# Loading 104 of 128 rows of keys and queries from the fifth unit of attention on

## The chip, the core and the metric

The kernel runs on one core of one Trainium2 chip, in one launch. The metric is the device time in microseconds (us). The core has a matrix engine (TensorE; PE in the profile, PEld for its weight loads), a vector engine (VectorE, DVE), a scalar engine (ScalarE, ACT), a general engine (GpSimd, POOL) and a queue processor that here only issues transfers (SyncE, SP). All transfers between the chip's memory and the core's own memory of 128 rows run on 16 DMA engines.

## The reference, cut to what matters

Three stages follow one another: a gated linear attention over 4 x 8 heads, 768 steps and 40 numbers a head; a routed layer of 8 experts with a capacity of 384 tokens each; and a dense layer with 2048 hidden units. The change touches the loads of the first.

```python
for t in range(S):
    kt, vt, qt = (k[:, :, t], v[:, :, t], q[:, :, t])
    ...
    C = f_stab[:, :, None, None] * C + i_stab[:, :, None, None] * np.einsum('bhd,bhe->bhde', vt, kt)
    n = f_stab[:, :, None] * n + i_stab[:, :, None] * kt
    h_tilde = np.einsum('bhde,bhe->bhd', C, qt)
    nq = np.einsum('bhd,bhd->bh', n, qt)[:, :, None]
    denom = np.maximum(np.abs(nq), 1.0)
    ...
    y[:, :, t] = o * h_tilde / denom
```

The attention's output, 3072 rows of 320, is routed to one of eight experts a row (`relu(x @ w1) @ w2`), and then goes through `elu(x @ w_in) @ w_out`.

## The kernel before

Attention is cut into 24 units: 12 chunks of 64 steps, times two pairs of batches. A unit holds 16 heads, 8 in the upper 64 rows and 8 in the lower 64 rows of every tile, since a head needs only 40 numbers. Its keys and queries are one tile `qk` of 128 rows x 2 x 8 x 64 numbers (512 KB): rows 0 to 39 carry one batch's 40 dimensions, rows 64 to 103 the other's. The host fills rows 40 to 63 and 104 to 127 with zeros (`_layout`, L1464 and L1465). The product of a unit's keys and queries (`scores`, L284) and of its scaled queries and the state (`recall`, L366) run over all 64 rows of a half, so what stands in those rows has to be zero.

There are four `qk` buffers (`QKb`, L149), used in turn. `load_qk` (L254) issues one transfer on the queue of SP. Units 0 to 3 are loaded at the start, unit 4 after the first scores, unit 5 in step 0. In step u the order of a unit is: 16 products of weights and values alternate on PE with 16 of the scores of unit u+2 (L352, L284); the decay factors of u+2 (L309, L299, L302); the transpose of the output of u-1 (L422); recall and the new state (L366, L378); on POOL the scaled queries of u+1 (`factors`, L316), which is the last reader of that unit's `qk` tile; then the load of unit u+5 into the same buffer, the gates on DVE and POOL (L398 to L406), the logits (L432), two writes of the output to memory (`rows_out`, L416) and the load of values and keys by token of unit u+4 (`load_vk`, L260, 484 KB).

So on SP's queue the transfers stand in a fixed order: two writes `xd`, one `vk`, now and then a piece of the dense layer's first weight (`cx`, L842, which is converted beside attention), one `qk`. A load that has to wait holds back all that stand behind it. The product of scores of unit u+5 comes in step u+3, over two steps after its load was issued. Units' loads number 24; the first four go to fresh buffers.

After attention come the routing rounds and, interleaved with them by a planner that works with fixed costs, the experts and the dense layer (L1081 and L1219 to L1223, the larger part of the time). They read nothing of `qk`.

Of the kernel before, what the change touches and what calls it, by code (L numbers as in the profile page):

```python
# [117 lines left out]
class Attention:  # L118
# [134 lines left out]

    def load_qk(self, u):  # L254
        self.QK[u] = self.QKb[u % 4]
        self.nc.sync.dma_start(self.QK[u], self.qk[u])

    def load_vk(self, u):
        self.VK[u] = self.two.tile([128, 968], F32, name="vk", bufs=6)
# [1237 lines left out]
```

## Time and profile before

| what | us |
|---|---|
| median of 3 runs | 794.91 |
| lowest and highest of them | 784.56, 798.31 |
| the profiled execution's own time | 790.17 |
| its span | 788.4 |

The profile is of one execution, with a mean granted clock of 0.944 for TensorE. It gives each engine's busy time, the share of the DMA engines that is busy, which engine waited for which, and the chain of work that ended last. Attention takes the first 160 us or so of the span, the routing alone some 30 us, the rest of the span is experts and dense layer.

### The profile page before, as it was taken

The numbers are of one execution on the slowest core, as the hardware profiler recorded it, in microseconds if no ns is written. First come the engines' busy times: TensorE is split into PE (matmuls) and PEld (weight loads), VectorE is DVE, ScalarE is ACT, GpSimd is POOL, SyncE is SP. The second block draws the span as 40 slices with busy tenths as digits, with TensorE's granted clock in tenths as the row PEclk, the third lists the DMA queues.
The fourth block names the chain that finished last, engine by engine and source line by source line (L and its number), as shares of the span: only waits on it lengthen the run. The fifth ranks groups of instructions, "written<-read, shape, count | busy, mean of one in ns | idle before, by whom it ended". The sixth has DMA issues, their size and how long they took to land.

```text
span 788.4 us, 18307 instructions
## 1 busy us (share of the span) xinstructions
PE 727.4 (92%) x7379; PEld 668.6 (85%) x7379; DVE 541.2 (69%) x1599; ACT 384.1 (49%) x822; POOL 222.8 (28%) x273
## 2 busy tenths in 40 slices
PE   7889789934999789999999999999999999999995
PEld 4767677823999688999999899999999999999994
DVE  8457657577889966795787579769857843852441
ACT  5545444424456643572565267336625743742452
POOL 4668757625213520121040012112012221001001
PEclk9879978966999889999999999999999999999998
DMA  7767777335212410230050023023002421000000
GB/s 272 240 207 253 248 234 215 94 98 174 92 29 64 154 59 1 74 105 26 1 177 2 25 81 98 26 81 97 1 26 82 135 72 58 35 1 26 1 1 26
DMA packets 24070, 72.80 MB, mean 92 GB/s; under 512 B 3568, under 2 KB 7664, under 8 KB 23984
## 3 DMA queue, kind: packets, MB, share of 16 engines
q1 hardware_dynamic: 15488, 39.80, 16.0%
q0 software_dynamic: 8448, 31.73, 12.3%
q8 instruction: 58, 0.95, 0.5%
q14 instruction: 28, 0.23, 0.1%
q10 hardware_dynamic: 48, 0.10, 0.0%
HBM read 62.96 MB, written 8.65 MB: 91 GB/s over the span
## 4 chain that ended last, share of the span: by engine, by line
PE 59%; issue 19%; POOL 8%; DVE 7%; DMA 3%; ACT 2%; SPq 1%; POOLq 0%; ACTq 0%; DVEq 0%
PE ph L1081 26%; PE acc L1223 5%; PE acc L1219 5%; PE acc L1220 5%; PE acc L1188 3%; PE acc L1190 2%; PE acc L1189 2%; POOL qt L316 2%; PE pr L713 2%; POOL kt L325 2%; POOL C L327 2%; PE acc L1175 1%; DMA qk<-in_qk_dram 1%; PE acc L1177 1%; PE pX L432 1%
## 5 line engine op out<-in xcount | busy, mean ns | idle before, releaser
L1219 PE MATMUL acc<-woh,gh 128*128 128x320 f32 x384 | 121.2, 315 | 1.5 <-ACT woh L958 1.5
L1223 PE MATMUL acc<-woh,gl 128*128 128x320 f32 x384 | 119.8, 312 | 0.7 <-DVE gl L965 0.6
L1220 PE MATMUL acc<-wol,gh 128*128 128x320 f32 x384 | 119.2, 311 | 0.5 <-POOL wol L951 0.5
L1130 ACT ACTIVATE e<-ph 128x384 f32<-128x384 f32 x128 | 62.3, 487 | 89.6 <-PE ph L1081 82.0
L1134 DVE SCALAR_TENSOR_TENSOR e<-e,ph 128x384 f32<-128x384 f32 x128 | 70.2, 550 | 49.7 <-ACT e L1131 49.4
L1081 PE MATMUL ph<-yh,wih 128*128 128x384 f32 x256 | 89.7, 351 | 0.3
L1098 ACT ACTIVATE gh<-ph 128x384 fp32r<-128x384 f32 x64 | 31.4, 490 | 116.6 <-PE ph L1081 100.0
L1081 PE MATMUL ph<-yh,wil 128*128 128x384 f32 x256 | 85.9, 335 | 0.0
L1229 POOL DMA_INDIRECT out_dram<-ot,idx x24 | 23.9, 996 | 202.5 <-ACT ot L958 199.7
L965 DVE TENSOR_TENSOR gl<-e,gh 128x384 fp32r<-128x384 f32 x128 | 73.4, 581 | 1.4
L1219 PEld LDWEIGHTS acc<-woh,gh 128*128 128x128 f32 x384 | 72.8, 190 | 1.8 <-ACT woh L958 1.8
L1223 PEld LDWEIGHTS acc<-woh,gl 128*128 128x128 f32 x384 | 72.6, 189 | 1.9 <-DVE gl L965 1.5
L1105 DVE SCALAR_TENSOR_TENSOR gl<-ph,gh 128x384 fp32r<-128x384 f32 x64 | 35.4, 555 | 56.1 <-ACT gh L1098 56.1
L1220 PEld LDWEIGHTS acc<-wol,gh 128*128 128x128 f32 x384 | 72.6, 189 | 0.8 <-POOL wol L951 0.8
L1131 ACT ACTIVATE e<-e 128x384 f32<-128x384 f32 x128 | 67.3, 526 | 4.1
L1081 PE MATMUL ph<-yl,wih 128*128 128x384 f32 x256 | 66.1, 339 | 0.0
L969 POOL DMA_INDIRECT stg<-in_w1a_dram,wi x16 | 16.3, 1018 | 145.9 <-DVE wi L751 128.2
L958 ACT ACTIVATE gh<-e 128x384 fp32r<-128x384 f32 x95 | 48.4, 515 | 11.2 <-DVE e L1134 11.0
L1081 PEld LDWEIGHTS ph<-yh,wih 128*128 128x128 f32 x256 | 48.3, 189 | 3.7 <-ACT yh L1193 3.6
L1081 PEld LDWEIGHTS ph<-yh,wil 128*128 128x128 f32 x256 | 48.2, 188 | 0.0
L1081 PE MATMUL ph<-xh,w1h 128*128 128x384 f32 x128 | 45.5, 355 | 0.7 <-ACT xh L958 0.6
L1081 PEld LDWEIGHTS ph<-yl,wih 128*128 128x128 f32 x256 | 45.8, 189 | 0.0
(260 smaller groups left out, 1929.7 us busy)
## 6 DMA issues: line engine op xcount, KB each, us to landing
qk<-in_qk_dram SPq DMA_DIRECT2D x24, 512.0 KB, 5.8
vk<-in_vk_dram SPq DMA_DIRECT2D x24, 484.0 KB, 4.5
wx<-in_wout_dram SPq DMA_DIRECT2D x16, 320.0 KB, 2.9
xd<-x SPq DMA_DIRECT2D x48, 96.0 KB, 2.3
cx<-in_win_dram SPq DMA_DIRECT2D x8, 512.0 KB, 5.7
cx<-in_win_dram SPq DMA_DIRECT2D x4, 256.0 KB, 6.4
xg<-xd,idx POOLq DMA_INDIRECT x24, 3.1
out_dram<-ot,idx POOLq DMA_INDIRECT x24, 2.5
```

The source lines that it names most:

```text
L958: self.nc.scalar.activation(out, x, AF.Copy)
L965: self.nc.vector.tensor_tensor(out, x, y, op=ALU.subtract)
L1081: PE.matmul(p, w, x, start=k == 0, stop=k == 7)
L1098: nc.scalar.activation(h, p, AF.Relu)
L1105: nc.vector.scalar_tensor_tensor(l, p, 0.0, h, op0=ALU.max, op1=ALU.subtract)
L1130: nc.scalar.activation(e, p, AF.Relu, scale=-1.0)
L1131: nc.scalar.activation(e, e, AF.Exp, scale=-1.0)
L1134: nc.vector.scalar_tensor_tensor(e, e, -1.0, p, op0=ALU.add, op1=ALU.max)
L1219: PE.matmul(p, h[:, c], self.woh[:, f], start=f == 0, stop=False)
L1220: PE.matmul(p, h[:, c], self.wol[:, f], start=False, stop=False)
L1223: PE.matmul(p, l[:, c], self.woh[:, f], start=False, stop=f == 15)
L1229: s = nc.gpsimd.indirect_dma_start(out=self.out, out_offset=bass.IndirectOffsetOnAxis(ap=idx[:, t:t + 1], axis=0), in_=o, in_offset=None)
```

## The change

From unit 4 on, a load takes rows 0 to 103 of the source and writes rows 0 to 103 of the buffer. Rows 104 to 127 of each of the four buffers keep what the first load wrote there, which is zeros. 20 of the 24 loads become 104 rows of 4096 bytes (416 KB) in place of 128 rows (512 KB). Nothing else changes: every engine has the same instructions in the same order as before, and the transfers wait for the same engines; only the size of these 20 differs.

```diff
     def load_qk(self, u):
         self.QK[u] = self.QKb[u % 4]
-        self.nc.sync.dma_start(self.QK[u], self.qk[u])
+        n = 128 if u < 4 else 104
+        self.nc.sync.dma_start(self.QK[u][:n], self.qk[u, :n])
```

## Rows read from the trace of the kernel before

**Rows 1.** The page: span, busy time of each engine with its share and instructions.

```profile
span 788.4 us, 18307 instructions
...
PE 727.4 (92%) x7379; PEld 668.6 (85%) x7379; DVE 541.2 (69%) x1599; ACT 384.1 (49%) x822; POOL 222.8 (28%) x273
```

**Rows 2.** The page: busy tenths in 40 slices, DMA engines and bytes moved likewise.

```profile
PE   7889789934999789999999999999999999999995
...
DMA  7767777335212410230050023023002421000000
```

**Rows 3.** Busy time by stretch: engines, granted clock, DMA share, GB/s; attention and four pieces.

```profile
core 0: us, PE busy (x) PEld busy (x) DVE busy (x) ACT busy (x) POOL busy (x), PEclk, DMA share, GB/s
15.00:141.00 126.00, 109.46 (x2909) 88.83 (x2908) 79.74 (x183) 61.52 (x141) 86.46 (x85) 0.84 0.71 224
48.00:59.00 11.00, 11.00 (x229) 8.96 (x229) 6.25 (x14) 5.41 (x12) 6.41 (x7) 0.53 0.73 235
59.00:89.00 30.00, 26.28 (x824) 21.40 (x818) 20.77 (x51) 15.35 (x39) 25.78 (x25) 1.00 0.79 257
107.00:117.00 10.00, 9.85 (x205) 8.14 (x208) 4.89 (x10) 4.06 (x11) 5.38 (x6) 0.51 0.84 249
130.00:141.00 11.00, 10.12 (x178) 8.15 (x178) 7.43 (x14) 4.53 (x10) 7.20 (x8) 0.53 0.56 179
```

**Rows 4.** The tile qk: who reads and writes it, when, and who waited for it.

```profile
L256 SPq DMA_DIRECT2D qk<-in_qk_dram x24: 327/390/2152, 1.2 to 132.3; - x24
L316 POOL TENSOR_TENSOR qt<-qk,db x22: 1286/1482/1814, 19.8 to 153.8; 128x512 f32<-128x512 f32 x22
...
who waited for it (us, times):
  PEld pS L284: 0.4, 1
...
DMA to landing us min/median/max: 4.0/5.8/9.2
```

**Rows 5.** SP's queue and PE in time: load of unit 12, its first product.

```profile
63.87 2.15 SPq L256 DMA_DIRECT2D qk<-in_qk_dram  x1
...
75.50 0.28 PE L284 MATMUL pS<-qk 64*64 64x64 f32 x2
```

**Rows 6.** DMA queues (packets, MB, share of 16 engines' span) and issues (KB each).

```profile
q1 hardware_dynamic: 15488, 39.80, 16.0%
...
q8 instruction: 58, 0.95, 0.5%
...
qk<-in_qk_dram SPq DMA_DIRECT2D x24, 512.0 KB, 5.8
vk<-in_vk_dram SPq DMA_DIRECT2D x24, 484.0 KB, 4.5
...
xd<-x SPq DMA_DIRECT2D x48, 96.0 KB, 2.3
cx<-in_win_dram SPq DMA_DIRECT2D x8, 512.0 KB, 5.7
cx<-in_win_dram SPq DMA_DIRECT2D x4, 256.0 KB, 6.4
```

**Rows 7.** The chain that ended last, 15 to 160 us: two of its longest pieces.

```profile
80.01 4.76 DMA qk<-in_qk_dram
105.22 5.17 DMA qk<-in_qk_dram
```

**Rows 8.** POOL in order of time, behind those two pieces of the chain.

```profile
83.28 1.74 POOL L316 TENSOR_TENSOR qt<-qk,db 128x512 f32<-128x512 f32 x1
84.99 1.26 POOL L914 TENSOR_TENSOR wil<-cF,wih 128x512 fp32r<-128x512 f32 x1
...
110.04 0.72 POOL L406 TENSOR_TENSOR x<-x,rd 128x320 f32<-128x320 f32 x1 [2.18 <-DVE x L405]
110.72 1.48 POOL L316 TENSOR_TENSOR qt<-qk,db 128x512 f32<-128x512 f32 x1
```

**Rows 9.** PE's waits, 15 to 160 us: us in total, times, longest.

```profile
PE pS L284 <- issue: 3.7, 3, 2.0
PE pO L352 <- issue: 2.6, 2, 2.5
PE pO L366 <- issue: 2.2, 1, 2.2
...
PE pF L309 <- issue: 1.4, 1, 1.4
```

**Rows 10.** PE in order of time: three of those waits, in brackets.

```profile
47.27 0.27 PE L284 MATMUL pS<-qk 64*64 64x64 f32 x2 [2.04 <-issue]
...
105.05 0.27 PE L352 MATMUL pO<-vk,P 64*64 64x64 f32 x2 [2.46 <-issue]
...
130.88 0.48 PE L284 MATMUL pS<-qk 64*64 64x64 f32 x4 [1.22 <-issue]
```

**Rows 11.** SP's own waits over the whole span.

```profile
SPq L416 <- ACT x L413: 83.5, 23, 6.9
```

## The prediction

> **What bounds the kernel now.** I read the page first. PE is busy for 92% of the span [rows 1], and from slice 19 on for nine tenths of every slice, while the DMA engines fall from seven tenths in the first slices to almost nothing [rows 2]. The experts and the dense layer behind attention are therefore PE's, and no load of keys and queries is left there. The change can act only on the first 155 us or so, and through the time at which attention ends.
>
> Next I read that stage by stretches [rows 3]. From 15 to 141 us no engine is full: PE is busy for 109.5 of 126 us, POOL for 86.5, VectorE for 79.7, and the DMA engines have a share of 0.71 at 224 GB/s. The pace comes from the 22 scaled-query instructions on POOL, the first at 19.8 and the last at 153.8 us [rows 4]: 134.0 / 21 = 6.4 us a unit. [...]
>
> Then I asked the tile itself who waits for its loads. In the whole run one instruction did, for 0.4 us, and it is a product of scores (L284) [rows 4]; the first loads of the program, which the change leaves alone, are those that nothing hides. Loads land 4.0 to 9.2 us after issue, 5.8 in the middle [rows 4]. Against that stands a lead of two steps: the load of unit 12 was held up longest on SP, was issued at 63.87, and its first product ran at 75.50 us [rows 5]. Even the slowest landing of all, 9.2 us, would have been there at 73.1.
>
> One view speaks against this. The chain of waits lists two qk loads, 4.76 and 5.17 us long, as pieces of the chain that ended last [rows 7]. What follows in the first case is POOL's L914, which reads no qk; POOL had been at work until then without a pause, as it had before L316 in the second [rows 8]. No engine stood still for these landings. The chain's steps are inferred from semaphores, and these two lead past an engine that was busy. I count them as no wait; were they real, the shorter load would give at most 24 of 128 rows of 9.9 us, 1.9 us.
>
> **The change, part by part.** It removes 20 x 24 rows of 4096 bytes, 1.97 MB. SP's queue carried 39.80 MB in 16.0% of 16 engines' span [rows 6], 0.16 x 16 x 788.4 = 2018 us of engine time, so 19.7 KB per us and engine. A load of 512 KB costs 26.6 us of engine time, 1.66 us on each of 16 engines; one of 416 KB costs 21.6, 1.35 us on each of 16. That is 20 x 0.31 = 6.2 us in all if the engines were the bound. They are not: at 0.71 they stand idle for more than a quarter of the stage. Its cover is the lead of two steps; were that gone, 0.31 us a unit is what it would be worth.
>
> By the rows an even spread, 1.35 us an engine, is the nearest guess, as every load shown has rows in multiples of 16. [...]
>
> SP issues the same number of transfers in the same order. Its issue of a qk load takes 390 ns in the middle [rows 4], and SP stands for 83.5 us of the run in front of the output's writes, waiting for ACT [rows 11]; even twice the 390 ns would disappear there. The engines' instructions and operands have the same shapes, so nothing is added to PE or POOL.
>
> What remains is contention. PE waits 9.9 us in this stage for nothing that the profile shows (3.7 + 2.6 + 2.2 + 1.4) [rows 9], in a few pieces of 1 to 2.5 us in the midst of products whose inputs are there; three stand in [rows 10], at 47, 105 and 131 us. Each of these three comes just before or at the start of a stretch at half clock. Those stretches hold 229 + 205 + 178 = 612 matmuls in 32 us, which take 22.3 us at 27.5 per us: 9.7 us lost. The DMA engines also carry 58 instruction packets, 0.95 MB, 0.5% of 16 engines' span [rows 6], so 16 KB and 1.1 us each, and these share the engines with the loads. [...]
>
> The price of less contention is bounded by 0 and by 9.9 + 9.7 = 19.6 us. The stage moves 24 x 512 + 24 x 484 + 48 x 96 + 8 x 512 + 4 x 256 = 33,632 KB [rows 6], and 20 x 96 = 1920 KB go, 5.7%. I take that share of the bound, 1.1 us, since only so much of the traffic leaves. Below nothing is not excluded either: where these waits fall differs from run to run, and the three runs of one program lie 13.75 us apart.
>
> **The sum.** 790.2 us of the profiled execution, less 1.1, is 789.1. That execution is 4.7 us under the median of the runs shown; from the median it is 793.8. I predict the middle of both, **792 us**.
>
> **Rivals.** [...]
>
> *The DMA engines are the bound after all.* Then the even spread gives 6.2 us, 784. Against it: the single wait of 0.4 us, and the lead. It lies within the forecast's range.
>
> *The 104 rows go to few engines, and the load becomes the bound.* All else takes 0.71 x 6.4 - 1.66 = 2.9 us of each engine a unit. With k engines the load adds 21.6 / k, and the unit grows once 2.9 + 21.6 / k passes 6.4, below k = 6.2. At 13 engines it is 4.6 and at 8 it is 5.6, both hidden; at 4 it is 8.3, and 1.9 us more for each of 20 units end at 828 us; one engine would give some 1,150. For it: no transfer with such a count of rows is shown. Against it: 104 can be cut evenly in 13 or 8 parts, and nothing in the rows confines a transfer to four.
>
> *The waits fall worse.* The same contention with other timing adds two or three waits of 2 us with their slow stretches, 6 to 14 us: 796 to 804, which is also the upper half of what the runs show.
>
> **How the numbers follow.** Forecast 0.80, with a range of its own of 781 to 802, which is the spread of the runs around it with the bounds of the small terms. PE's waits gone (under 781) 0.09, few engines 0.05, worse waits beyond 802 0.06. 2% of the median, 15.9 us, is about what a measurement of this kernel can tell from no change; it puts the limits at 779 and 811. Of the first rival 0.07 lies under 779; of the last 0.01 lies over 811, with the 0.05 of few engines. So faster 0.07, same 0.87, slower 0.06. The range 778 to 804 leaves out the far ends of each.
>
> **What would show it.** The qk load's time to landing should stay between 4 and 9 us, with 5 or so in the middle, and nobody should wait for it beyond the start. The DMA share from 15 to 141 us should fall by a few hundredths, not the unit's 6.4 us. [...] Only a stage that gets shorter while no wait of PE's has changed would break the reasoning as a whole.

## The result and the profile after

The change makes the kernel a little slower: 797.93 us in the median of 20 runs (792.7 to 803.8) against 795.01 us of before (20 runs, 784.56 to 800.89), ratio 1.0063 with a 95% interval of 1.0038 to 1.0087. The ratio leaves out seven runs of before that took over 1.5% longer than its fastest, and none of the change; over all 20 and 20 the medians stand at 1.0037, the means at 1.0037 with an interval of 1.001 to 1.0066. I had forecast a little faster.

The profiled execution took 799.42 us, its span is 797.7 us, 9.3 us longer than before. The medians differ by 2.9 us only, so the two profiles show more than the change costs. PE's busy time is that of [rows 1], 727.8 against 727.4 us.

The tile qk and its users (as [rows 4]): count, shortest, middle and longest in ns, first and last start in us.

```profile
L257 SPq DMA_DIRECT2D qk<-in_qk_dram x24: 318/366/1409, 1.2 to 140.4; - x24
L317 POOL TENSOR_TENSOR qt<-qk,db x22: 1281/1484/1753, 19.4 to 162.0; 128x512 f32<-128x512 f32 x22
...
who waited for it (us, times):
busy tenths in 40 slices 9999999900000000000000000000000000000000
```

The last scaled-query instruction starts at 162.0 in place of 153.8 us: 8.2 of the 9.3 us were lost inside attention. Nobody waited for a qk load; before, one instruction did, for 0.4 us [rows 4]. The lead of two steps held, so the loss did not come by a late load.

PE's waits from 15 us to the end of attention (as [rows 9]): us in total, times, longest.

```profile
PE pC L379 <- issue: 6.8, 3, 2.9
PE pS L285 <- issue: 6.0, 3, 3.1
PE pO L367 <- issue: 5.0, 3, 2.2
PE pD L310 <- issue: 3.2, 1, 3.2
...
PE pO L353 <- issue: 1.0, 2, 0.8
```

The waits for nothing that the profile shows went from 9.9 us (10.3 with two of 0.2 us that [rows 9] does not show) to 22.0 us. In these two executions that is the whole loss, and more. Three of them in order of time, with the wait in brackets:

```profile
49.46 0.37 PE L285 MATMUL pS<-qk 64*64 64x64 f32 x2 [3.14 <-issue]
...
77.43 0.53 PE L310 MATMUL pD<-fp,sel 96*128 96x64 bf16 x7 [3.19 <-issue]
...
120.38 0.43 PE L379 MATMUL pC<-vk,kt 64*40 64x64 f32 x2 [2.88 <-issue]
```

They are not only more but longer: 3.1 and 3.2 us where the longest in [rows 9] was 2.5.

The DMA queues (as [rows 6]) and the stretch 15 to 141 us (as [rows 3]; the last three numbers are granted clock, DMA share and GB/s):

```profile
q1 hardware_dynamic: 14948, 37.83, 16.5%
```

```profile
15.00:141.00 126.00, 99.73 (x2696) 81.18 (x2695) 74.62 (x173) 56.97 (x132) 81.79 (x80) 0.85 0.72 201
```

This is the surprise. SP's queue moved 1.97 MB less and kept the engines busy for longer: 0.165 x 16 x 797.7 = 2106 us of engine time against 2018, 55.7 us per MB against 50.7. In the same 126 us the DMA share is 0.72 (before 0.71) at 201 GB/s (before 224), and PE got 2696 matmuls done in place of 2909, at a granted clock of 0.85 against 0.84. So it is not the clock.

The packets' own records in the trace say which ones became slow. All 4096-byte packets of SP's queue (qk and cx) and the 3872-byte ones (vk), from 16 us to the end of attention:

```
                 4096 bytes: mean ns, share over 200 ns     3872 bytes: mean ns
before           179, 0.11                                  209
change           221, 0.46                                  211
```

The 3872-byte packets, of loads that were not cut, stay as they were. The 4096-byte ones are those of qk and cx together. Counted off in the order of the issues, which is an estimate where two transfers overlap, qk's took 173 ns before and 232 after, cx's 189 and 203, and cx's smaller packets of 1024 bytes 74 and 96. So the cut loads became slower most, and cx a little with them.

The queue has 540 packets fewer (14948 against 15488), the 480 rows and three more for each of the 20 loads. These three are packets of 4 bytes: 2016 of them before, 16 for each of the queue's 126 transfers, and 1956 after, so 13 for a load of 104 rows. I take them for one on each engine that carries rows of the load, 13 engines in place of 16; that is an estimate from these counts, since no record names its engine. The trace also has 40 completions fewer on SP's semaphores, two for each of the 20 loads.

### The profile page after: what moved, and what is told of

It reads as the page before. It is cut to its first block, busy times and chain, and to the rows that moved or that the text cites. A ratio compares the mean times of both kernels' runs of the same rounds, so it can differ in the third digit from the quotient of the medians.

```text
span 797.7 us, 18307 instructions
## 1 busy us (share of the span) xinstructions
PE 727.8 (91%) x7379; PEld 669.0 (84%) x7379; DVE 540.7 (68%) x1599; ACT 384.0 (48%) x822; POOL 223.3 (28%) x273
## 3 DMA queue, kind: packets, MB, share of 16 engines
q1 hardware_dynamic: 14948, 37.83, 16.5%
## 4 chain that ended last, share of the span: by engine, by line
PE 64%; issue 19%; DVE 7%; POOL 5%; ACT 2%; DMA 1%; SPq 0%; POOLq 0%; DVEq 0%
PE ph L1082 26%; PE acc L1224 5%; PE acc L1220 5%; PE acc L1221 5%; PE acc L1189 3%; PE acc L1191 2%; PE acc L1190 2%; PE pO L353 2%; PE pr L714 2%; PE pX L433 2%; POOL qt L317 1%; PE acc L1176 1%; PE pO L367 1%; PE acc L1178 1%; POOL C L328 1%
```

## Experiments

All were timed in several rounds beside the kernel before. "Waits" are the sums of PE's waits without a releaser in attention; engine time is the share of SP's queue x 16 x span. The two come from one profiled execution each, the ratio from the timed runs. The versions with 96, 16 and 64 rows and the last one of all leave out rows that hold data and compute other numbers; the part behind the last scaled-query instruction is 634 to 638 us long in every one of the profiles, so they did not shorten it by that.

**Other counts of rows.** Is it the 13 engines of that estimate, or any cut?

```diff
-        n = 128 if u < 4 else 104
+        n = 128 if u < 4 else 112      # 120, 96 and 16 in the others
```

Expected of 112 rows: 

> From unit 4 on, a load takes 112 rows in place of 104 (of before: 128). Theory A (engines): what cost time is that 104 rows can only be cut evenly in 13, so that 13 engines carry a load and slow one another's packets; 112 is 16 times 7. Then engine time per MB on SP's queue is back at some 50 us (before 50.7, change 55.7), TensorE's waits without a releaser are back near 10 us (before 9.9, change 22), and the time is that of before or a little under: ratio 0.992 to 1.002. Theory B (fewer rows): any load that is cut short does it, by its length or by writing a part of the tile; 16 of 24 rows are saved here, so some two thirds of the loss: ratio about 1.004, waits 16 to 20 us.

Expected of 120 rows: 

> From unit 4 on, a load takes 120 rows. Theory A: 120 is 15 times 8, so 15 engines carry it, out of step with the transfers that use 16, and their packets slow down as with 13: 53 to 57 us of engine time per MB, waits 14 to 25 us, ratio 1.002 to 1.010, although only 8 rows of 128 are saved. Theory B: a third of the loss, ratio about 1.002, waits 12 to 14 us.

Expected of 96 rows: 

> From unit 4 on, a load takes 96 rows; rows 96 to 103 keep the numbers of units 0 to 3, so 8 of 40 dimensions of two batches are those of an older unit. Theory A: 16 engines with 6 rows each, 50 us of engine time per MB, waits at or under 10 us, ratio 0.990 to 1.001. Theory B: a third more is saved than by the change, so a third more is lost: ratio about 1.008, waits 20 to 27 us.

Expected of 16 rows: 

> From unit 4 on, a load takes 16 rows, one an engine; the other rows keep the numbers of units 0 to 3. A third of attention's traffic is gone (448 of 1400 KB a unit). Theory A, its second half (TensorE's waits are for code whose packets stand behind the loads' on the same engines): waits fall under 5 us, fewer stretches run at half clock, ratio 0.975 to 0.992. Rival C (the waits have nothing to do with the loads): waits stay at 8 to 12 us, ratio 0.996 to 1.004.

SP's queue in these four, in this order (packets, MB, share of 16 engines' span; spans 790.9, 795.1, 787.3 and 781.7 us):

```profile
q1 hardware_dynamic: 15168, 38.49, 16.6%
```

```profile
q1 hardware_dynamic: 15308, 39.15, 17.5%
```

```profile
q1 hardware_dynamic: 14848, 37.18, 16.3%
```

```profile
q1 hardware_dynamic: 13248, 30.63, 13.3%
```

Measured ratios: 112 rows 1.0007 (0.998 to 1.0034), 120 rows 1.0106 (1.0069 to 1.0143), 96 rows 1.0001 (0.996 to 1.0042), 16 rows 0.982 (0.9776 to 0.9865). Theory B falls: 120 rows leave out least and cost most. Theory A has its times nearly right and its reason wrong. At 112 and 96 rows all 16 engines work by the same estimate (320 and 640 packets fewer than before, the rows and no others), and yet the engine time per MB is 54.6 and 55.2 us, near the change's 55.7 and not the 51 that is left when rows at 179 ns are taken out; the 4096-byte packets take 213 and 212 ns, with 120 rows 244. What these two save in rows they lose again in slow packets. The engine time of SP's queue, 2101, 2226, 2053 and 1663 us against 2018, orders the dearest and the cheapest of them rightly; 112 rows should have cost some and cost nothing that can be measured.

The waits came out as theory A had them for none of these: 16.2 us with 112 rows and 16.7 with 96, where it had some 10, and only 12.9 with 120, the slowest kernel of all. Those of 112 and 120 rows lie in theory B's ranges, whose times failed. The loss with 120 rows shows in the granted clock instead, 0.81 from 15 to 149 us, where the change has 0.85 and 112 and 96 rows have 0.89:

```profile
15.00:149.00 134.00, 113.59 (x2946) 92.01 (x2946) 79.77 (x183) 62.48 (x143) 86.09 (x85) 0.81 0.77 208
```

With 16 rows the packets take 181 ns and the waits are 8.1 us, not under 5 as expected, and inside what rival C had; the time, 0.982, is the one that theory A's second half had.

**Where the rows lie.** The same number of rows and bytes, in two places of the tile; and all 128 rows in two halves. Theory P (places) has the place of the rows set how long a packet takes, theory Q (counts) their number.

```diff
-        self.nc.sync.dma_start(self.QK[u], self.qk[u])
+        a, b = (0, 128) if u < 4 else (32, 96)      # the other is the change with 64 in place of 104
+        self.nc.sync.dma_start(self.QK[u][a:b], self.qk[u, a:b])
```

```diff
-        self.nc.sync.dma_start(self.QK[u], self.qk[u])
+        for a, b in ([(0, 128)] if u < 4 else [(0, 64), (64, 128)]):      # (0, 48), (64, 112) in the other
+            self.nc.sync.dma_start(self.QK[u][a:b], self.qk[u, a:b])
```

Expected of rows 0 to 63: 

> From unit 4 on, a load takes rows 0 to 63 alone, 4 rows an engine on 16 engines; the lower half keeps the numbers of units 0 to 3. [...] Theory Q (counts): the slowing comes from the number of rows an engine or from their number in all; then this run and the run of rows 32 to 95 agree in packets and time. By the runs so far the time changes by 0.6 of the change in the busiest engine's time: P gives 0.990 to 0.998, Q 0.986 to 0.994.

Expected of rows 32 to 95: 

> [...] P: packets of 4096 bytes at 160 to 175 ns in the mean, engine time per MB near 50 us, ratio 0.984 to 0.993, below the other run. Q: no difference between the two in packets or time.

Expected of 48 and 48 rows: 

> From unit 4 on, two transfers a unit, of rows 0 to 47 and 64 to 111: 96 rows, 3 and 3 an engine on 16 engines, nothing left out but zeros. If the time follows the busiest engine's time: 6 packets of some 200 ns are 1.2 us a unit against 1.33 of before, so 20 x 0.13 x 0.6 = 1.6 us less, ratio 0.993 to 1.003 with one more issue on SP. If a second transfer a unit costs of itself (issue, completion), 1.004 or more.

Expected of 64 and 64 rows: 

> From unit 4 on, all 128 rows, but in two transfers, rows 0 to 63 and 64 to 127, 4 rows an engine each: no byte less than before. P: packets over 200 ns, some 1.7 us an engine and unit against 1.33, ratio 1.002 to 1.010, slower than before although nothing was cut. Theory B or Q (cut loads cost): packets and time as before, ratio 0.998 to 1.002.

SP's queue and the landing of qk loads (issues: KB each, median us to landing), first rows 0 to 63, then rows 32 to 95:

```profile
q1 hardware_dynamic: 14208, 34.56, 15.2%
...
qk<-in_qk_dram SPq DMA_DIRECT2D x20, 256.0 KB, 5.5
```

```profile
q1 hardware_dynamic: 14208, 34.56, 14.4%
...
qk<-in_qk_dram SPq DMA_DIRECT2D x20, 256.0 KB, 4.9
```

Packet for packet and byte for byte the same, and 0.152 x 16 x 791.7 = 1925 against 0.144 x 16 x 782.9 = 1804 us of engine time. The 4096-byte packets take 220 ns in the mean in the first and 179 in the second, where 0.10 of them take over 200 ns, as before the change. The ratios are 0.994 (0.9898 to 0.9982) and 0.9869 (0.982 to 0.9917), the medians 787.79 and 783.35 us, PE's waits 15.9 and 8.6 us. The intervals of the ratios just overlap, and the packets decide: theory Q falls, P stands, the place of the rows set how long a packet took, 220 against 179 ns. Why one place is slower than the other was not shown: the trace doesn't have which engine takes which rows.

All 128 rows in two halves:

```profile
q1 hardware_dynamic: 15808, 39.80, 17.9%
```

```profile
15.00:141.00 126.00, 102.30 (x2781) 83.70 (x2777) 76.00 (x178) 59.64 (x138) 81.19 (x80) 0.86 0.83 225
```

The bytes are those of before, the engine time is 0.179 x 16 x 793.7 = 2273 us, the DMA share 0.83, the packets 246 ns, the waits 20.3 us, the ratio 1.004 (1.0008 to 1.0073). Nothing was cut, and the kernel loses, if a little less than with the change. By the engine time alone it should have lost more.

48 and 48 rows gave 0.9985 (0.995 to 1.0021): 2065 us of engine time, packets of 225 ns, waits of 14.5 us. As many rows in one transfer (0 to 95) gave 1.0001, so a second transfer a unit costs nothing that can be measured.

**Versions of 80 rows, and the bulk of the traffic taken away.** The first shifts the upper half's data to rows 24 to 63, with 24 columns of zeros put ahead of the keys by token, so that all data stand in rows 24 to 103, and loads these 80 rows by one transfer; its control shifts them and loads 128 rows.

```diff
...
-        self.nc.sync.dma_start(self.QK[u], self.qk[u])
+        a, b = (0, 128) if u < 4 else (24, 104)      # (0, 128) always in the control
+        self.nc.sync.dma_start(self.QK[u][a:b], self.qk[u, a:b])
...
+            m, c = (40, h * 40 + 24) if r else (64, h * 40)
+            self.nc.tensor.matmul(self.pC[r:r + m, h], kt[r:r + 64, c:c + m], self.value(u, h, r), start=True, stop=True)
...
-    d["qk"][:, :, :40] = np.stack([by_dim(i[n]) for n in ("k", "q")], 4)
+    x = np.stack([by_dim(i[n]) for n in ("k", "q")], 4)
+    d["qk"][:, 0, 24:], d["qk"][:, 1, :40] = x[:, 0], x[:, 1]
```

```diff
-        self.nc.sync.dma_start(self.QK[u], self.qk[u])
+        for a, b in ([(0, 128)] if u < 4 else [(0, 40), (64, 104)]):
+            self.nc.sync.dma_start(self.QK[u][a:b], self.qk[u, a:b])
```

```diff
+        n = 128 if u < 4 else 16      # keys and queries
...
+        n = 128 if u < 6 else 16      # values and keys by token, in six fixed buffers
+        self.nc.sync.dma_start(self.VK[u][:n], self.vk[u, :n])
```

Expected of rows 24 to 103: 

> [...] If the time follows the busiest engine's time: 5 packets of 165 to 190 ns are 0.9 us a unit against 1.33 of before, 20 x 0.45 x 0.6 = 5 us less, ratio 0.986 to 0.997, TensorE's unexplained waits at or under 10 us. If any cut other than 128 rows (or 64 from row 32) collides: packets over 210 ns, ratio 0.995 to 1.002.

Expected of its control: 

> The control for the 80-row version: the same layout with data in rows 24 to 103, the same products for the state (64 columns of weights in place of 40 in the upper half), but all 128 rows loaded by one transfer as before. Layout alone costs nothing: ratio 0.998 to 1.003, packets as before. If the wider products cost: 1.003 or more.

Expected of 40 and 40 rows: 

> From unit 4 on, two transfers a unit, rows 0 to 39 and 64 to 103, nothing left out but zeros: 80 of 128 rows. [...] Theory A (busiest engine): 1.3 to 1.6 us a unit on it, ratio 0.999 to 1.005. Rival V (volume): 37% of the rows are gone, ratio under 0.995.

Expected with both loads cut to 16 rows: 

> From unit 4 on 16 rows of keys and queries, and from unit 6 on 16 rows of values and keys by token, one row an engine each; all other rows keep the numbers of earlier units. Two thirds of attention's traffic are gone. If TensorE's unexplained waits come from traffic in front of what it waits for: under 4 us, ratio 0.965 to 0.980. If a remainder of 8 us (as with 16 rows of keys and queries alone) has another cause: 7 to 9 us stay, ratio 0.978 to 0.986.

Rows 24 to 103 (960 packets fewer than before, the rows and no others, so by the estimate 5 rows on each of 16 engines) gave 0.9959 (0.9924 to 0.9994), its control 0.9978 (0.9939 to 1.0016): as expected in time, though with waits of 14.8 us and packets between clean and slow (197 ns), and with intervals that overlap. The control has the loads of before, and its packets are those of before (179 ns); its waits are 11.9 us against 10.3, so one profile tells a difference of a few us from none only in part. 40 and 40 rows gave 0.992 (0.9881 to 0.9959), 785.33 us. This is the fastest kernel that computes everything, and theory A (busiest engine) falls with it: by the estimate 10 engines of 16 carry these loads (1200 packets fewer than with 64 and 64 rows, the 960 rows and six more for each of the 40 transfers), 8 rows each, as many as before. Its queue and its stretch:

```profile
q1 hardware_dynamic: 14608, 35.87, 15.3%
```

```profile
15.00:141.00 126.00, 110.26 (x3163) 91.23 (x3161) 86.18 (x197) 65.33 (x153) 90.41 (x90) 0.88 0.69 205
```

Its packets take 196 ns, between clean and slow, and there are 37% fewer of them: 1910 us of engine time, waits of 8.4 us. Fewer rows with packets that were not too slow paid off here.

With both loads cut to 16 rows, PE's waits without a releaser, all of them, then the stretch, the scaled queries and SP's queue:

```profile
PE pO L369 <- issue: 1.5, 1, 1.5
...
PE pX L435 <- issue: 0.8, 1, 0.8
...
PE pS L287 <- issue: 0.2, 1, 0.2
```

```profile
15.00:141.00 126.00, 114.02 (x3442) 94.24 (x3442) 90.54 (x221) 68.72 (x165) 96.64 (x94) 0.96 0.40 108
...
L319 POOL TENSOR_TENSOR qt<-qk,db x22: 1290/1488/1755, 20.0 to 134.0; 128x512 f32<-128x512 f32 x22
...
q1 hardware_dynamic: 11232, 22.82, 10.3%
```

2.5 us of waits remain, the granted clock is 0.96, PE does 3442 matmuls in the stretch where the kernel before did 2909, and the ratio is 0.9751 (0.9705 to 0.9797). The last scaled queries start at 134.0 in place of 153.8 us, and what follows them lasts 637.3 us against 634.6 before, so the time was gained in attention. With the bulk of the traffic the waits went, from 22.0 us with the change and 8.1 with 16 rows of keys and queries: that the loads cause most of them is shown.

## Why the prediction was wrong

The sign was wrong: 1.1 us less were forecast, and the kernel lost 0.63%, 2.9 us by the medians. 797.93 us lies inside the range, on the side of its last rival; that it does is the width of the range and no merit of the sum. (The middle of 789.1 and 793.8 is 791.5; I wrote 792.)

- *What bounds the kernel, and the lead.* Right. No instruction that reads the tile waited for a qk load after the start in any run, the two pieces of qk on the chain were no waits, and the part behind attention kept its length. In the three runs with two transfers a unit the profile puts waits on a qk load, 9.2 us with 48 and 48 rows, but of instructions on POOL and ACT that work on `x` and not on `qk`.
- *The engine time of a load.* **This step failed.** I took 19.7 KB per us and engine from all of SP's queue and applied it to another shape: a load was to fall from 26.6 to 21.6 us of engine time. It did not fall. With the mean of the 4096-byte packets it went from 128 x 179 ns = 22.9 us to 104 x 221 ns = 23.0 us, from 1.43 us on each of 16 engines to 1.77 on each of the estimate's 13, where I had 1.35 by an even spread over 16; the 21.6 us over 13 are 1.66. With qk's own packets as counted above, 173 and 232 ns, it rose from 22.2 to 24.1 us. The queue's total rose by 88 us instead of falling by 100: by some 55 in the 4096-byte packets, though there are 480 fewer, by some 23 in cx's packets of 1024 bytes, and by little things. The even spread was my guess from loads with rows in multiples of 16, and the 13 small packets of a load speak against it. The larger error is the packets' time: at 179 ns 104 of them are 18.6 us. The runs at rows 0 to 63 and 32 to 95 show a packet's time change with the place of the rows, 220 and 179 ns; the reason was not shown.
- *The term of contention.* The mechanism was the right one to price, and its sign followed from the failed step. PE's unexplained waits are few where packets are clean or few (10.3 us before, 8.6 with rows 32 to 95, 8.1 with 16 rows, 2.5 with hardly any) and most with the change (22.0) and with 128 rows in two halves (20.3). In between they do not go in step with the time: 16.2 and 16.7 us with 112 and 96 rows, which lost nothing, and 12.9 with 120, which lost most and has the lowest clock. The 27.5 matmuls per us in the bound are 824 in 30 us, at a granted clock of 1.00 [rows 3]. I scaled the 19.6 us with the bytes, 5.7% less; the engine time, 4.4% more (2106 / 2018), would have given the sign, but with 0.9 us not the size. The second half of the bound, slow clock after the waits, stayed where it was in this execution (0.85 against 0.84).
- *The rivals.* "PE's waits gone", the first rival of the chances, did not come: they rose from 10.3 to 22.0 us. The few engines came only as the estimate's 13, which hide a load: nobody waited for one (the profile after gives no times to landing). That the DMA engines are the bound as they are priced there, 6.2 us faster, did not come either. "The waits fall worse" gave 796 to 804 and is what happened, but for a cause I had not named: not other timing alone, but slower packets. So the hit of this rival's times was luck.
- *What would show it.* The test I set, a DMA share that falls by a few hundredths, failed at once: 0.72 after 0.71.

Across the runs the time follows the engine time of SP's queue roughly: from 2018 to 1663 us (16 rows) 1.8% or 14.3 us were gained, 0.64 us for each us of all 16 engines. By that line the change's 88 us cost 0.64 x 5.5 = 3.5 us, against 5.0 by the ratio and 2.9 by the medians, and 120 rows 8.3 against 8.4; but 128 rows in two halves should have cost 10 and cost 3.2, and 112 rows 3.3 and cost 0.6. It is a guide and no law. Whether 13 and 15 engines add something of their own is open: 104 and 112 rows have the same engine time (2106 and 2101 us), and their intervals just miss each other.

The packets' records point to what PE waits for in these pieces. The instruction packets of q8, 16 KB each, come every 5 to 6 us in attention; 58 of them over PE's 2 x 7379 products and weight loads would be 64 bytes an instruction, an estimate that takes all of q8 for PE's. The three waits shown above, and the packet of q8 that ended last before each wait's end:

```
wait, us              packet of q8, us      from the packet's end to the wait's end
46.32 to 49.46        46.79 to 47.99        1.5
74.24 to 77.43        74.52 to 75.83        1.6
117.50 to 120.38      117.14 to 118.68      1.7
```

All twelve waits of this profile end 1.2 to 1.7 us after such a packet, and so do all 120 waits of 0.3 us or more in the fourteen profiles (1.21 to 1.70 us). Waits for something else would hardly keep that distance. I read it as PE standing still until its code had arrived, as the second half of theory A has it; that is my estimate from these distances, and the profile names no releaser. How slower or more loads make the code late stays open: the records don't have the time at which a packet was asked for, and no run took the code away.

## What to carry to other kernels

Here a transfer's price went with its packets' time, not with its bytes (1.97 MB less, 88 us of engine time more): after a cut, look at the queue's engine time (its share x 16 x span) and at the mean time of packets of one size before trusting the saving. The time per MB alone misleads: it is 55.7 us with the change, and 54.3 and 55.7 in the two fastest versions, whose queue works for 1663 and 1271 us. Leaving out rows of a full 128-row load made the queue's work dearer (2018 us of engine time before, 2226 with 120 rows); if rows are to go, compare several cuts, here 40 and 40 rows (0.992) against 104 in one (1.0063). A load that nobody waits for can still cost time through what it delays elsewhere: PE's waits without a releaser rose from 10.3 to 22.0 us, by my estimate for its own code.

## What the runs showed of the hardware

The same 64 rows' worth of bytes cost 1925 us of the queue's engine time at rows 0 to 63 and 1804 us at rows 32 to 95, with 4096-byte packets of 220 and 179 ns. Two halves of 64 rows in place of one transfer of 128 rows took the packets from 179 to 246 ns. And with the change TensorE stood still for 22 us of attention without waiting for any engine or any data that the profile shows, in pieces that each end 1.2 to 1.7 us after a 16 KB packet of instructions; with two thirds of the loads' traffic gone, 2.5 us of that were left.
